# Attention, cosine network and top-1 experts: the gate in column groups, the sinks as one product, the masks first

## The chip, the cores and the metric

The kernel runs on one core of one Trainium2 chip. The metric is the device time of an execution in microseconds (us), as the median of several runs. Five engines work side by side, each on its own queue of instructions: PE multiplies matrices (PEld is its weight load), DVE, ACT and POOL work on vectors, and SP starts transfers.

## What is computed

```python
def _attn_ref(q, k, v, n_sink, window):          # 4 batches, 8 heads, 768 x 64
    scores = scale * np.matmul(q, k.transpose(0, 1, 3, 2))
    keep = is_sink | in_window                   # 4 sinks, a window of 128
    scores = np.where(keep, scores, -1000000000.0)
    a = softmax(scores)
    return np.matmul(a, v)

x = attn_out.transpose(0, 2, 1, 3).reshape(3072, 512)
h = x @ w_in                                     # 512 -> 2048
x = (h * np.cos(h)) @ w_out                      # 2048 -> 512
logits = x @ w_gate + modality_bias[modality_id] # 8 experts
e_idx = np.argmax(logits, axis=1)
out[mask] = gate_w[mask, None] * (np.maximum(x[mask] @ w1[e], 0.0) @ w2[e])   # expert by expert
```

## The kernel before

Attention goes by half-batches hb = 0 to 7 of 384 queries (an even hb is the first half of its batch) and in each by 4 pairs of heads. `attn_front` (L395) makes a pair's generators. The front loads queries and keys, transposes them on PE and has ACT copy them out of PSUM (L450, L468). `mid` (L474) multiplies them (tile ps), lets DVE add the masks and find the maxima (L502), and ACT take exponents (L518). `rest` (L521) scales and transposes the probabilities (pt, pT) and multiplies them with the values into po. Window and sinks are apart there: the sinks' probabilities, 16 columns a head, are copied to pc (by POOL for the first half-batches, then by DVE, L573, L575), transposed into pz (L578), copied by ACT into sp (L579), and multiplied with the sinks' values vs_n, one product for each head, into the two halves of po's partitions (L592). From hb = 2 on (`whole`) this runs beside the first network; from hb = 3 (`STACK`) the scores are three products of split operands in fp32r.

The first network, `ffn_tile_gen` (L648), goes by tiles of 384 tokens and 16 blocks of 128 hidden columns: 12 matmuls hp with 384 columns, a cosine on DVE and ACT (ch), and 9 matmuls y with 512 columns, in fp32r, each operand split in a high and a low part (g_h and g_l, the latter made on POOL, L699). `conv_gen` (L274) builds such parts of the weights out of 64-bit inputs on ACT and DVE during the first 200 us.

For each finished tile of y, `route_tile` (L734) chooses the experts. For each of its 3 blocks of 128 tokens PE transposes the block (yT, L743), DVE copies it out, and PE multiplies it with the gate's weights: 4 products of 128 rows with 8 moving columns (pl, L754). These are woven between matmuls of the first network (`mmf`, L625). DVE adds the bias and goes on to ranks and lists. Eight tiles give 24 blocks. After it come the experts, in pages of 256 tokens, under branches (`run`, L1291).

A scheduler sorts the instructions of each engine by priority and dependences; edges between instructions (`add_manual_dep`) restrain it. The start of the program, L842 to L954, was written thus: front of the first pair, transfers of sinks and window (L849), masks (L886 to L904) and the routing's constants (L906 to L940), the first weight conversion, the rest of the first pair.

Of the kernel before, what the change touches and what calls it, by code (L numbers as in the profile page):

```python
# [11 lines left out]
F32 = DT.float32  # L12
# [45 lines left out]
CONV_LEAD = 8  # L58


@with_exitstack
def kernel(
# [178 lines left out]
    sp2 = [apool.tile([P, HALF], F32, name=f"sp{i}") for i in range(2)]  # L241
# [14 lines left out]

    def conv_bits(cpool, raw):
# [3 lines left out]
        ACT.activation(out=h, in_=hi.bitcast(F32), func=AF.Copy, scale=REBASE)  # L261
# [133 lines left out]
    def attn_front(hb, pr):  # L395
# [10 lines left out]

        vs_n, sp = vs_n2[pr % 2], sp2[pr % 2]
# [59 lines left out]
        else:  # L467
            ACT.activation(out=kT[0][:, 0:nblk, 0:P], in_=pk3[:, 0:nblk, :], func=AF.Copy)  # L468
# [52 lines left out]
        def rest():  # L521
# [47 lines left out]
            pc = apool.tile([P, NQ, 2, NS], F32, name="pc")  # L569
            if extra:  # L570
# [3 lines left out]
            else:  # L574
                (POOL if hb < NPOOL else DVE).tensor_copy(pc[:, t0:], Pt[:, t0:, :, P:SEG])  # L575
            pz = psb("pz")
            for t in range(t0, NQ):
                PE.transpose(pz[0:2 * NS, t * P:(t + 1) * P], pc[:, t].rearrange("p j s -> p (j s)"), ident)  # L578
            ACT.activation(out=sp[0:2 * NS, t0 * P:], in_=pz[0:2 * NS, t0 * P:HALF], func=AF.Copy)  # L579
# [11 lines left out]
            for j in range(2):  # L591
                mm(po[hr[j], t0 * P:HALF], vs_n[:, j * D:(j + 1) * D], sp[:, t0 * P:HALF], True, False)  # L592
# [27 lines left out]
    woven = []  # L620

    edge = mybir.DependencyInfo(mybir.DependencyClass.NoSync, mybir.DependencyReason.DATA)
    last_mm = [None]

    def mmf(o, l, r, start, stop):  # L625
        i = PE.matmul(o, l, r, start=start, stop=stop)  # L626
        if last_mm[0] is not None:
            tc.add_manual_dep(i.ins, last_mm[0].ins.name, edge, reason="woven")
            last_mm[0] = None
        if woven:  # L630
            last_mm[0] = woven.pop(0)()
            tc.add_manual_dep(last_mm[0].ins, i.ins.name, edge, reason="woven")

    def weave():
        if woven:
            woven.pop(0)()


# [9 lines left out]
    def ffn_tile_gen(ypool_of):  # L648
# [4 lines left out]
        def second(c):  # L653
# [6 lines left out]
            for t in range(NQ):  # L660
                yp = yps[i][t]
                s = slice(t * P, (t + 1) * P)
                mmf(yp, gh[:, s], oh, f == f0, False)
                mmf(yp, gh[:, s], ol, False, False)
                mmf(yp, gl[:, s], oh, False, f == f1 - 1)
# [68 lines left out]
    def route_tile(i, yp):  # L734
# [3 lines left out]
        lg = yp.tile(s3, F32, name="lg")  # L738
        for t in range(NQ):
# [4 lines left out]
            yT = yp.tile([P, KD, P], F32, name="yT", bufs=1)  # L744
            DVE.tensor_copy(yT.rearrange("p c x -> p (c x)"), pt)
            yield 0
            for _ in range(4 if i < NTILE - 2 else 0):
                yield 0
            pl = []

            def gate(c):
                if c == 0:
                    pl.append(ps_a("pl"))
# [4 lines left out]
            while woven:  # L758
                weave()
            tt(DVE, lg[:, t, :], pl[0][:, 0:NE], bias_all[:, t0 + t, :], ALU.add)  # L760
            if t < NQ - 1:
                continue
            yield 0
# [78 lines left out]
    first = attn_front(0, 0)  # L842
    next(first)
    next(first)

# [3 lines left out]
    SP.dma_start(out=rt[:, 0:2], in_=n_sink.partition_broadcast(P).squeeze(1))  # L849
    SP.dma_start(out=rt[:, 2:4], in_=window.partition_broadcast(P).squeeze(1))  # L850
# [15 lines left out]
    bad = tmpc.tile([P, 2], F32, name="bad")  # L866
    ts(DVE, bad[:, 0:1], ns_c, float(NS), ALU.is_gt)
    ts(DVE, bad[:, 1:2], win_c, float(P), ALU.is_gt)
    tt(DVE, bad[:, 0:1], bad[:, 0:1], bad[:, 1:2], ALU.add)
    ts(DVE, bad[:, 1:2], win_c, 1.0, ALU.is_lt)  # L870
    tt(DVE, bad[:, 0:1], bad[:, 0:1], bad[:, 1:2], ALU.add)
    bad_i = const.tile([P, 1], I32, name="bad_i")
    DVE.tensor_copy(bad_i, bad[:, 0:1])


    iota_i = tmpc.tile([P, NV], I32, name="iota_i")
    POOL.iota(iota_i, pattern=[[1, NV]], base=0, channel_multiplier=0)
    iota_f = const.tile([P, NV], F32, name="iota_f")
    DVE.tensor_copy(iota_f, iota_i)
    prow_i = tmpc.tile([P, 1], I32, name="prow_i")  # L880
    POOL.iota(prow_i, pattern=[[0, 1]], base=0, channel_multiplier=1)
    cols2 = const.tile([P, 2], F32, name="cols2")
    prow, half_pi = cols2[:, 0:1], cols2[:, 1:2]
    DVE.tensor_copy(prow, prow_i)

    masks = const.tile([P, 3, W3], BF16, name="masks")  # L886
    rel = tmpc.tile([P, P], F32, name="rel")
    sk = tmpc.tile([P, P], F32, name="sk")
    mw = tmpc.tile([P, P], F32, name="mw")
    ts(DVE, rel, iota_f[:, 0:P], prow, ALU.subtract, -1.0, ALU.mult)  # L890
    ts(DVE, sk, iota_f[:, 0:P], ns_c, ALU.is_lt)
    POOL.memset(masks, 0.0)

# [10 lines left out]
    ts(DVE, masks, masks, -1.0, ALU.add, -NEG / SCALE, ALU.mult)  # L904

    sides = const.tile([P, 2, P], BF16, name="sides")  # L906
    ts(DVE, sides[:, 0], rel, 0.0, ALU.is_gt)
    ts(DVE, sides[:, 1], rel, 0.0, ALU.is_le)
    tri = const.tile([P, P], BF16, name="tri")
    ones = const.tile([P, P], BF16, name="ones")  # L910
    ts(DVE, tri, rel, 0.0, ALU.is_lt)
    DVE.memset(ones, 1.0)
    DVE.memset(half_pi, HALF_PI)

    wg = const.tile([P, KD, NE], F32, name="wg")
# [478 lines left out]
```

## Time and profile before

| | |
|---|---|
| three runs | 1146.69, 1145.22, 1146.74 us; median 1146.69 |
| the profiled execution | 1143.94 us, its span 1142.2 |
| PE busy | 1103.6 us, 97% of the span, 6624 matmuls |
| DVE, ACT, POOL busy | 678.3 us (59%), 602.5 (53%), 224.5 (20%) |
| mean granted clock of PE | 0.996 |

Busy time is the union of an engine's instructions. Those of PE overlap in the records, so what one costs is read from the start of one to the start of the next. Line numbers are those of the kernel before. Idle time of an engine costs something only where others wait for it.

### The profile page before, as it was taken

How to read it: one execution, taken by the hardware profiler on the slowest of the kernel's cores; microseconds unless marked ns; L12 is line 12 of the kernel's file. 1: busy time of each engine (PE TensorE's matmuls, PEld its weight loads, DVE VectorE, ACT ScalarE, POOL GpSimd, SP SyncE). 2: the span in 40 equal slices, each digit the busy share in tenths (PEclk: the TensorE clock that was granted, in tenths of full speed). 3: DMA queues.
4: the chain of work that ended last, by engine and by line, in shares of the span. 5: the costliest groups of instructions: out<-in, count | busy, mean ns of one | idle time of the engine just before them, and what ended most of it. 6: DMA issues, size and time to landing. Idle time of an engine off the chain costs nothing.

```text
span 1142.2 us, 20840 instructions
## 1 busy us (share of the span) xinstructions
PE 1103.6 (97%) x6624; PEld 928.0 (81%) x6624; DVE 678.3 (59%) x2126; ACT 602.5 (53%) x1239; POOL 224.5 (20%) x273
## 2 busy tenths in 40 slices
PE   5989999999999999999999999999999999999995
PEld 3667777888888878888888879999889998899984
DVE  6778888666876766776676774746742125522210
ACT  5878887656665566665657553434322225422221
POOL 1232224211111111111111111322121211221110
PEclk9999999999999999999999999999999999999998
DMA  6567665422332322323233223633151115111110
GB/s 150 151 197 196 195 195 158 109 73 68 95 74 76 105 72 64 108 70 75 63 104 79 62 75 102 230 93 89 60 203 40 57 58 184 41 58 39 40 43 23
DMA packets 136083, 113.40 MB, mean 99 GB/s; under 512 B 95727, under 2 KB 103919, under 8 KB 135920
## 3 DMA queue, kind: packets, MB, share of 16 engines
q1 hardware_dynamic: 131600, 97.87, 30.3%
q0 software_dynamic: 4320, 13.65, 3.7%
q8 instruction: 66, 1.08, 0.4%
q14 instruction: 97, 0.79, 0.2%
HBM read 151.06 MB, written 19.67 MB: 149 GB/s over the span
## 4 chain that ended last, share of the span: by engine, by line
PE 85%; DVE 5%; DMA 5%; ACT 2%; issue 1%; POOL 1%; SPq 0%; DVEq 0%; POOLq 0%; ACTq 0%
PE hp L136 23%; PE y L626 22%; PE m_h L136 10%; PE m_y L136 10%; PE ps L136 5%; PE po L136 5%; DMA out_dram<-m_ot,m_ids 3%; DMA cv_in<-in_moe_w_in_dram 1%; PE pl L754 1%; PE pq L444 1%; PE pt L546 1%; PE yT L743 1%; PE pk L454 1%; PE m_a L1093 1%; PE mh L136 1%
## 5 line engine op out<-in xcount | busy, mean ns | idle before, releaser
L148 POOL TENSOR_TENSOR g_l<-ch,g_h 128x384 fp32r<-128x384 f32 x128 | 132.4, 1035 | 558.2 <-ACT g_h L698 435.4
L136 PE MATMUL hp<-xT_h,wi_h 128*128 128x384 f32 x512 | 188.3, 368 | 2.7 <-DVE ch L148 2.7
L136 PE MATMUL hp<-xT_h,wi_l 128*128 128x384 f32 x512 | 174.5, 341 | 0.0
L136 PE MATMUL hp<-xT_l,wi_h 128*128 128x384 f32 x512 | 174.0, 340 | 0.0
L626 PE MATMUL y<-wo,g_h 128*128 128x512 f32 x384 | 158.6, 414 | 0.0
L626 PE MATMUL y<-wo_l,g_h 128*128 128x512 f32 x384 | 155.6, 405 | 0.0
L626 PE MATMUL y<-wo,g_l 128*128 128x512 f32 x384 | 154.1, 401 | 0.2 <-POOL g_l L148 0.2
L688 ACT ACTIVATE ch<-ch,cols 128x384 f32<-128x384 f32 x128 | 78.7, 616 | 116.6 <-DVE ch L145 116.0
L136 PE MATMUL m_y<-wi_h,hT 128*128 128x512 f32 x416 | 132.5, 393 | 0.7 <-ACT m_ot L1135 0.6
L145 DVE SCALAR_TENSOR_TENSOR hT<-m_h,hT 128x256 fp32r<-128x256 f32 x88 | 37.3, 424 | 151.0 <-ACTq L1287 102.4
L136 PEld LDWEIGHTS hp<-xT_h,wi_h 128*128 128x128 f32 x512 | 96.7, 189 | 18.1 <-issue 7.2
L142 DVE TENSOR_SCALAR ch<-hp 128x384 int32<-128x384 f32 x128 | 70.9, 554 | 59.1 <-PE hp L136 46.3
L698 ACT ACTIVATE g_h<-ch 128x384 fp32r<-128x384 f32 x128 | 66.4, 520 | 67.8 <-DVE ch L148 46.0
L136 PEld LDWEIGHTS hp<-xT_l,wi_h 128*128 128x128 f32 x512 | 97.0, 189 | 3.7 <-issue 0.2
L136 PEld LDWEIGHTS hp<-xT_h,wi_l 128*128 128x128 f32 x512 | 96.7, 189 | 1.2 <-issue 0.9
L148 DVE TENSOR_TENSOR ch<-ch,hp 128x384 f32<-128x384 f32 x128 | 70.4, 550 | 39.9 <-ACT ch L688 39.5
L136 PEld LDWEIGHTS m_y<-wi_h,hT 128*128 128x128 f32 x416 | 78.1, 188 | 17.0 <-issue 1.0
L518 ACT ACTIVATE Pb<-Pb,mx 128x272 f32<-128x272 f32 (+1 forms) x168 | 82.9, 494 | 10.9 <-DVE mx L502 10.0
L626 PEld LDWEIGHTS y<-wo,g_l 128*128 128x128 f32 x384 | 72.2, 188 | 14.8 <-POOL g_l L148 0.8
L626 PEld LDWEIGHTS y<-wo,g_h 128*128 128x128 f32 x384 | 72.4, 189 | 13.8 <-issue 3.3
L502 DVE CUSTOM_DVE_ANT_0 Pb<-ps,masks 128x272 f32<-128x272 f32 (+1 forms) x168 | 63.7, 411 | 31.7 <-PE ps L136 31.2
L136 PE MATMUL ps<-kT,qT 64*128 64x272 f32 (+1 forms) x504 | 72.6, 350 | 8.9 <-ACT kT L468 7.0
(276 smaller groups left out, 2236.0 us busy)
## 6 DMA issues: line engine op xcount, KB each, us to landing
rw<-in_moe_w_dram SPq DMA_DIRECT2D x112, 512.0 KB
wo_l<-wl_scr SPq DMA_DIRECT2D x122, 256.0 KB
cv_in<-in_moe_w_in_dram SPq DMA_DIRECT2D x16, 512.0 KB
cv_out<-in_moe_w_out_dram SPq DMA_DIRECT2D x16, 512.0 KB
y_scr<-yt SPq DMA_DIRECT2D x24, 256.5 KB
xT_h<-xg_h SPq DMA_DIRECT2D x32, 192.0 KB
xT_l<-xg_l SPq DMA_DIRECT2D x32, 192.0 KB
qn<-in_q_dram SPq DMA_DIRECT2D x56, 96.0 KB
```

Source lines behind the costliest of these rows:

```text
L136: PE.matmul(o, l, r, start=start, stop=stop)
L142: e.tensor_scalar(out=o, in0=i, scalar1=s1, scalar2=s2, op0=op0, op1=op1)
L145: e.scalar_tensor_tensor(out=o, in0=i0, scalar=s, in1=i1, op0=op0, op1=op1)
L148: e.tensor_tensor(out=o, in0=a, in1=b, op=op)
L444: PE.transpose(pq[:, t * P:(t + 1) * P], qn[:, t].rearrange("p j d -> p (j d)"), ident)
L454: PE.transpose(pk[:, t * P:(t + 1) * P], kn[:, t].rearrange("p j d -> p (j d)"), ident)
L502: DVE.tensor_tensor_reduce(out=Pb[t][j][:, c0:c1], in0=ps[j][:, 0:w], in1=masks[:, min(half * NQ + t, 2), c0:c1], scale=-SCALE, scalar=3.0 ...
L518: ACT.activation(out=Pb[t][j][:, c0:c1], in_=Pb[t][j][:, c0:c1], func=AF.Exp, scale=-1.0, bias=mx[:, i:i + 1], accum_out=sm[:, i:i + 1])
L546: PE.transpose(pt2[:, j * P:(j + 1) * P], Pb[t][j][:, SEG:W3], ident)
L626: i = PE.matmul(o, l, r, start=start, stop=stop)
L688: ACT.activation(out=ch, in_=ch, func=AF.Sin, scale=TWO_PI, bias=half_pi)
L698: ACT.activation(out=gh, in_=ch, func=AF.Copy)
```

## The change

It has three parts, and a small fourth.

The gate: a tile's three transposed blocks go into one tile yT of 4 x 384 columns. The weights are widened to 32 columns with zeros and become the stationary side: four fp32 products with 384 moving columns, each into 32 partitions of one PSUM tile (pg). ACT copies that out, and three products with 8 columns against a matrix of ones (gsum) add up the four parts and turn them. Weaving goes.

The sinks, for hb from 2 on: DVE splits pc into high, high and low parts (96 rows after the transpose), POOL makes high, low and high parts of the values, and one fp32r product of all 128 columns gives what two fp32 products gave.

The start: masks ahead of all other work on DVE, in a fixed order; the sinks' and window's words loaded by ACT; the first pair finished behind the masks; the first conversion on ACT behind the first keys; all other constants behind half-batch 0.

The fourth: the hint of an expert page's branch goes to ACT and DVE too.

```diff
+            if whole:
+                pc = apool.tile([P, NQ, 3, 2, NS], F32R, name="pc3")
+                pv = Pt[:, t0:, :, P:SEG]
+                DVE.tensor_copy(pc[:, t0:, 0:2], pv.unsqueeze(2).to_broadcast([P, NQ - t0, 2, 2, NS]))
+                tt(DVE, pc[:, t0:, 2], pv, pc[:, t0:, 0].bitcast(F32), ALU.subtract)
+                vsr = vsr2[pr % 2]
+                i0, i1, i2 = [slice(i * 2 * NS, (i + 1) * 2 * NS) for i in range(3)]
+                POOL.tensor_copy(vsr[i0], vs_n[i0])
+                POOL.tensor_copy(vsr[i2], vs_n[i0])
+                tt(POOL, vsr[i1], vs_n[i0], vsr[i0].bitcast(F32), ALU.subtract)
...
-            ACT.activation(out=sp[0:2 * NS, t0 * P:], in_=pz[0:2 * NS, t0 * P:HALF], func=AF.Copy)
+            ACT.activation(out=sp[0:nr, t0 * P:], in_=pz[0:nr, t0 * P:HALF], func=AF.Copy)
...
-            for j in range(2):
+            if whole:
+                mm(po[:, t0 * P:HALF], vsr2[pr % 2], sp[:, t0 * P:HALF], True, False)
+            for j in range(0 if whole else 2):
                 mm(po[hr[j], t0 * P:HALF], vs_n[:, j * D:(j + 1) * D], sp[:, t0 * P:HALF], True, False)
...
-                mmf(yp, gh[:, s], oh, f == f0, False)
+                mm(yp, gh[:, s], oh, f == f0, False)
...
-            DVE.tensor_copy(yT.rearrange("p c x -> p (c x)"), pt)
+            DVE.tensor_copy(yT[:, :, t * P:(t + 1) * P], pt.rearrange("p (c x) -> p c x", x=P))
             yield 0
...
-                return PE.matmul(pl[0][:, 0:NE], yT[:, c, :], wg[:, c, :], start=c == 0, stop=c == KD - 1)
-
-            woven.extend([lambda c=c: gate(c) for c in range(KD)])
...
+        pg_ = ps_a("pg")
+        for c in range(KD):
+            mm(pg_[c * GW:(c + 1) * GW, 0:HALF], wg[:, c, :], yT[:, c, :], True, True)
+        gs = yT[:, 0, :]
+        ACT.activation(out=gs, in_=pg_[:, 0:HALF], func=AF.Copy)
+        yield 0
+        pl = ps_a("pl")
+        for t in range(NQ):
+            mm(pl[:, t * NE:(t + 1) * NE], gs[:, t * P:(t + 1) * P], gsum, True, True)
+        tt(DVE, lg, pl[:, 0:NQ * NE].rearrange("p (t e) -> p t e", e=NE), bias_all[:, t0:t0 + NQ, :], ALU.add)
...
-    SP.dma_start(out=rt[:, 0:2], in_=n_sink.partition_broadcast(P).squeeze(1))
-    SP.dma_start(out=rt[:, 2:4], in_=window.partition_broadcast(P).squeeze(1))
+    ACT.dma_start(out=rt[:, 0:2], in_=n_sink.partition_broadcast(P).squeeze(1))
+    ACT.dma_start(out=rt[:, 2:4], in_=window.partition_broadcast(P).squeeze(1))
...
+    made = DVE.tensor_scalar(out=masks, in0=masks, scalar1=-1.0, scalar2=-NEG / SCALE, op0=ALU.add, op1=ALU.mult)
+    mine = [i_ for i_ in nc.cur_bb.bb.instructions[at_:] if i_.engine == made.ins.engine]
+    for a_, b_ in zip(mine, mine[1:]):
+        tc.add_manual_dep(b_, a_.name, nosync, reason="masks in this order")
+
+    with tc.issue_after(made.ins):
+        first = attn_front(0, 0)
...
+        next(conv)
+        fronts[0, 0][0]()
...
+    with tc.issue_after([i_ for i_ in nc.cur_bb.bb.instructions if i_.engine == made.ins.engine][-1]):
+        sides = const.tile([P, 2, P], BF16, name="sides")
...
-                tc.mark_branch_hint_location(f"full{T + 1}", hint=flags[T + 1, "full"], engines=(ET.PE,))
+                tc.mark_branch_hint_location(f"full{T + 1}", hint=flags[T + 1, "full"], engines=(ET.PE, ET.Activation, ET.DVE))
```

Three places show how instructions move. The first is DVE's queue at the program's start, before: `rel`, `sk` and `mw` are masks in the making, `m`, `btmp`, `sides` and `tri` constants of the routing and of later half-batches, `ks` the first pair's sink keys.

```order
L140 TENSOR_SCALAR sk<-iota_f,lim 128x128
L142 TENSOR_SCALAR rel<-iota_f,cols_198 128x128
L148 TENSOR_TENSOR btmp<-m_233,mb 128x192
L140 TENSOR_SCALAR mw<-rel,lim 128x128
L903 CAST masks<-sk 128x16
L140 TENSOR_SCALAR sides<-rel 128x128
L145 SCALAR_TENSOR_TENSOR mw<-rel,mw 128x128
L458 COPY ks<-pk 128x16
L896 CAST masks<-mw 128x128
L897 CAST masks<-mw 128x128
L148 TENSOR_TENSOR masks<-mw,sk 128x128
```

After the change, in the same place, down to the first reduction of scores:

```order
L900 CAST masks<-mw 128x128
L149 TENSOR_TENSOR masks<-mw,sk 128x128
L902 CAST masks<-sk 128x16
L903 TENSOR_SCALAR masks<-masks 128x816
L472 COPY ks<-pk 128x16
L141 TENSOR_SCALAR bad<-lim 128x1 x2
L149 TENSOR_TENSOR bad<-bad 128x1
L141 TENSOR_SCALAR bad<-lim 128x1
L149 TENSOR_TENSOR bad<-bad 128x1
L486 COPY kT<-pk 128x2x16
L924 CAST bad_i<-bad 128x1
L518 ISA Pb,mx<-ps,masks 128x128
```

The masks stand without constants between them, and the first pair's keys and the test of the inputs (`bad`) behind them.

The second is DVE's queue at the end of half-batch 0, before, where `xs` is the last pair's scaling and `pb_x` a reduction of half-batch 1's scores:

```order
L502 ISA Pb,mx<-ps,masks 128x272
L502 ISA mx 128x1
L148 TENSOR_TENSOR xs<-po,xs 128x384
L145 SCALAR_TENSOR_TENSOR cv_a<-cv_h,cv_a 128x512
L140 TENSOR_SCALAR sm<-sm 128x6
L470 COPY kT<-ks 128x3x16
L563 RECIPROCAL sm<-sm 128x6
L145 SCALAR_TENSOR_TENSOR cv_a<-cv_out,cv_a 128x512
L502 ISA pb_x_98,mx<-ps,masks 128x272
L502 ISA mx 128x1
```

After:

```order
L149 TENSOR_TENSOR xs<-po,xs 128x384
L141 TENSOR_SCALAR sides<-rel 128x128 x2
L141 TENSOR_SCALAR tri<-rel 128x128
L951 MEMSET ones 128x128
L956 CAST m_1097<-mid 128x24
L143 TENSOR_SCALAR tok_1103<-iota_f 128x24
L967 MEMSET wg 128x4x24
L143 TENSOR_SCALAR m_1097<-m_1097 128x24
L149 TENSOR_TENSOR btmp<-m_1097,mb 128x192
L149 TENSOR_TENSOR bias_all<-m_1097,mb 128x192
L141 TENSOR_SCALAR tok_1103<-tok_1103,cols_161 128x24
L149 TENSOR_TENSOR bias_all<-bias_all,btmp 128x192
```

The constants have come in between, as one block.

The third is PE's queue behind the last tile of the first network, before, where `mh` are matmuls of the first expert's page:

```order
L136 MATMUL mh<-m_xT_l,wi_h_79 128x256
L754 MATMUL pl<-wg,yT 128x8 x4
L136 MATMUL mh<-m_xT_h,wi_l_89 128x256
L136 MATMUL mh<-m_xT_h,wi_h_80 128x256
L136 MATMUL mh<-m_xT_l,wi_h_80 128x256
L743 MATMUL yT<-ident,yt 128x128 x4
L136 MATMUL mh<-m_xT_h,wi_l_90 128x256
L136 MATMUL mh<-m_xT_h,wi_h_81 128x256
L754 MATMUL pl<-wg,yT 128x8 x4
L136 MATMUL mh<-m_xT_l,wi_h_81 128x256
L136 MATMUL mh<-m_xT_h,wi_l_91 128x256
```

After:

```order
L137 MATMUL mh<-m_xT_l,wi_h_81 128x256
L137 MATMUL mh<-m_xT_h,wi_l_91 128x256
L137 MATMUL pg<-yT,wg 32x384 x4
L137 MATMUL mh<-m_xT_h,wi_h_78 128x256
L137 MATMUL mh<-m_xT_l,wi_h_78 128x256
L137 MATMUL mh<-m_xT_h,wi_l_88 128x256
L137 MATMUL mh<-m_xT_h,wi_h_79 128x256
L137 MATMUL mh<-m_xT_l,wi_h_79 128x256
L137 MATMUL pl<-gsum,yT 128x8 x3
L137 MATMUL mh<-m_xT_h,wi_l_89 128x256
```

Three groups of four small products (the rows show two of them) have become four wide ones and three small ones, with five matmuls between.

## Rows read from the trace of the kernel before

**Rows 1.** Two stretches: busy us (instructions) of PE, PEld, DVE, ACT, POOL; clock, DMA share, GB/s
```profile
200.00:700.00 500.00, 498.58 (x3024) 413.23 (x3024) 346.22 (x1154) 307.28 (x604) 86.45 (x85) 1.00 0.31 83
830.00:1142.00 312.00, 295.61 (x1847) 265.19 (x1846) 93.43 (x260) 89.30 (x193) 54.01 (x51) 0.99 0.22 72
```

**Rows 2.** Timeline of the start: start us, us, engine, line, operation, tiles, idle before
```profile
3.36 0.43 SPq L850 DMA_DIRECT2D rt<-in_window_dram  x1
...
5.21 0.88 PE L454 MATMUL pk<-ident,kn 128*128 128x128 f32 x3
5.34 2.80 SPq L249 DMA_DIRECT2D cv_in<-in_moe_w_in_dram  x2
7.01 0.17 DVE L852 CAST rf<-rt 128x4 f32<-128x4 int32 x1 [5.47 <-DMA rt<-in_window_dram]
...
11.58 0.66 ACT L261 ACTIVATE cv_h<-cv_in 128x512 f32<-128x512 f32 x1 [9.54 <-DMA cv_in<-in_moe_w_in_dram]
...
12.52 0.48 ACT L468 ACTIVATE kT<-pk 128x384 f32<-128x384 f32 x1
...
13.05 1.08 PE L136 MATMUL ps<-kT,qT 64*128 64x128 f32 x4 [6.96 <-ACT kT L468]
13.14 0.36 DVE L142 TENSOR_SCALAR masks<-masks 128x816 bf16<-128x816 bf16 x1
...
14.92 0.28 DVE L502 CUSTOM_DVE_ANT_0 Pb<-ps,masks 128x128 f32<-128x128 f32 x1
```

**Rows 3.** Timeline of PE round one gate block of the last tile
```profile
817.49 0.28 PE L136 MATMUL mh<-m_xT_h,wi_h 128*128 128x256 f32 x1
817.61 0.96 PE L754 MATMUL pl<-wg,yT 128*128 128x8 f32 x8
818.43 0.36 PE L136 MATMUL mh<-m_xT_l,wi_h 128*128 128x256 f32 x1
818.63 0.28 PE L136 MATMUL mh<-m_xT_h,wi_l 128*128 128x256 f32 x1
```

**Rows 4.** Timeline of PE round the sinks of an odd half-batch's pair
```profile
225.23 0.39 PE L626 MATMUL y<-wo_l,g_h 128*128 128x512 f32 x1
225.46 0.40 PE L626 MATMUL y<-wo,g_l 128*128 128x512 f32 x1
225.79 0.87 PE L136 MATMUL po<-sp,vs_n 128*64 128x384 f32 x4
226.49 1.47 PE L136 MATMUL po<-pT,vn 128*64 128x128 f32 x16
227.88 0.45 PE L136 MATMUL hp<-xT_h,wi_h 128*128 128x384 f32 x1
228.17 0.34 PE L136 MATMUL hp<-xT_l,wi_h 128*128 128x384 f32 x1
228.34 0.33 PE L136 MATMUL hp<-xT_h,wi_l 128*128 128x384 f32 x1
```

**Rows 5.** Timeline of PE at the sinks of an even half-batch's pair
```profile
131.09 0.44 PE L136 MATMUL po<-sp,vs_n 128*64 128x128 f32 x4
131.36 1.03 PE L136 MATMUL po<-pT,vn 128*64 128x256 f32 x6
```

**Rows 6.** Timeline of PE at the first cosines
```profile
66.20 0.44 PE L136 MATMUL hp<-xT_h,wi_h 128*128 128x384 f32 x1 [2.73 <-DVE ch L148]
...
67.03 0.52 PE L136 MATMUL hp<-xT_l,wi_h 128*128 128x384 f32 x1
67.35 0.52 PE L136 MATMUL hp<-xT_h,wi_l 128*128 128x384 f32 x1
```

**Rows 7.** The tiles pc and g_l: instructions, ns min/median/max, first and last start
```profile
L575 DVE COPY pc<-Pb x20: 181/194/226, 221.1 to 681.6; 128x96 f32<-128x96 f32 x12, 128x32 f32<-128x32 f32 x8
...
L575 POOL COPY pc<-Pb x8: 208/212/349, 21.5 to 194.8; 128x32 f32<-128x32 f32 x6, 128x96 f32<-128x96 f32 x2
...
L148 POOL TENSOR_TENSOR g_l<-ch,g_h x128: 995/1012/1549, 67.1 to 809.2; 128x384 fp32r<-128x384 f32 x128
```

More of the change, by code (lines that the diff above doesn't have):

```diff
@@ L240 @@
     vs_n2 = [apool.tile([P, 2 * D], F32, name=f"vs_n{i}") for i in range(2)]
-    sp2 = [apool.tile([P, HALF], F32, name=f"sp{i}") for i in range(2)]
+    sp2 = [apool.tile([P, HALF], F32, name=f"sp{i}", tag=f"sp{i}") for i in range(2)]
+    vsr2 = []
     for i in range(2):
@@ L260, in conv_bits @@
         h = cpool.tile([P, 512], F32, name="cv_h", bufs=2)
-        ACT.activation(out=h, in_=hi.bitcast(F32), func=AF.Copy, scale=REBASE)
+        i_ = ACT.activation(out=h, in_=hi.bitcast(F32), func=AF.Copy, scale=REBASE)
+        if front_act:
+            tc.add_manual_dep(i_.ins, front_act[-1].ins.name, nosync, reason="behind the first keys")
+            front_act.clear()
         h = h.bitcast(I32)
@@ L405, in folded @@
             return whole and (half == 1 or t > 1)
+        if whole and not vsr2:
+            for i in range(2):
+                vsr2.append(apool.tile([P, 2 * D], F32R, name=f"vs_r{i}"))
+                sp2[i] = apool.tile([P, HALF], F32R, name=f"sp_r{i}", tag=f"sp{i}")
+                POOL.memset(vsr2[i].bitcast(F32), 0.0)
+                POOL.memset(sp2[i].bitcast(F32), 0.0)
         vs_n, sp = vs_n2[pr % 2], sp2[pr % 2]
@@ L467, in attn_front @@
         else:
-            ACT.activation(out=kT[0][:, 0:nblk, 0:P], in_=pk3[:, 0:nblk, :], func=AF.Copy)
+            i_ = ACT.activation(out=kT[0][:, 0:nblk, 0:P], in_=pk3[:, 0:nblk, :], func=AF.Copy)
+            if hb == 0 and pr == 0:
+                front_act.append(i_)
             src = pk3[:, 0:1, 0:NS] if half == 0 else ks[:, pr, 0:1, :]
@@ L848 @@
     rt = tmpc.tile([P, 4], I32, name="rt")
-    SP.dma_start(out=rt[:, 0:2], in_=n_sink.partition_broadcast(P).squeeze(1))
-    SP.dma_start(out=rt[:, 2:4], in_=window.partition_broadcast(P).squeeze(1))
+    ACT.dma_start(out=rt[:, 0:2], in_=n_sink.partition_broadcast(P).squeeze(1))
+    ACT.dma_start(out=rt[:, 2:4], in_=window.partition_broadcast(P).squeeze(1))
+    iota_i = tmpc.tile([P, NV], I32, name="iota_i")
+    POOL.iota(iota_i, pattern=[[1, NV]], base=0, channel_multiplier=0)
+    prow_i = tmpc.tile([P, 1], I32, name="prow_i")
+    POOL.iota(prow_i, pattern=[[0, 1]], base=0, channel_multiplier=1)
+    masks = const.tile([P, 3, W3], BF16, name="masks")
+    POOL.memset(masks, 0.0)
+    at_ = len(nc.cur_bb.bb.instructions)
+    iota_f = const.tile([P, NV], F32, name="iota_f")
+    DVE.tensor_copy(iota_f, iota_i)
+    cols2 = const.tile([P, 2], F32, name="cols2")
+    prow, half_pi = cols2[:, 0:1], cols2[:, 1:2]
+    DVE.tensor_copy(prow, prow_i)
+    rel = tmpc.tile([P, P], F32, name="rel")
+    sk = tmpc.tile([P, P], F32, name="sk")
+    mw = tmpc.tile([P, P], F32, name="mw")
+    ts(DVE, rel, iota_f[:, 0:P], prow, ALU.subtract, -1.0, ALU.mult)
     rf = tmpc.tile([P, 4], F32, name="rf")
@@ new lines @@
+    mine = [i_ for i_ in nc.cur_bb.bb.instructions[at_:] if i_.engine == made.ins.engine]
[3 more added lines that the diff above has]
+        first = attn_front(0, 0)
+        for _ in first:
+            pass
+        mids.add((0, 0))
+        for _ in fronts[0, 0][1]():
+            pass
+        next(conv)
+        fronts[0, 0][0]()
+        bad = tmpc.tile([P, 2], F32, name="bad")
+        ts(DVE, bad[:, 0:1], ns_c, float(NS), ALU.is_gt)
+        ts(DVE, bad[:, 1:2], win_c, float(P), ALU.is_gt)
+        tt(DVE, bad[:, 0:1], bad[:, 0:1], bad[:, 1:2], ALU.add)
+        ts(DVE, bad[:, 1:2], win_c, 1.0, ALU.is_lt)
+        tt(DVE, bad[:, 0:1], bad[:, 0:1], bad[:, 1:2], ALU.add)
+        bad_i = const.tile([P, 1], I32, name="bad_i")
+        DVE.tensor_copy(bad_i, bad[:, 0:1])
```

152 lines of the change are left out of this document (53 added, 99 removed).

## The prediction

> **What bounds the kernel now.** I read the table by stretches first. Between 200 and 700 us PE is busy for 498.6 of 500 us, DVE for 346, ACT for 307, POOL for 86 [rows 1]. Attention and the first network share PE there, and the other engines have a third of their time free: what leaves PE shortens this stretch, what is added to the others is covered. In the last 312 us, the experts, PE is busy for 295.6 [rows 1]; none of the changed matmuls are there. Then the timeline of the first 16 us: PE ends its transposes of the first keys at 6.1, and does nothing until 13.05, when ACT has copied them out [rows 2]. ACT could have copied at 6.1; it stood at the first weight conversion, whose data landed at 11.58 [rows 2]. Even without that, the first scores wait for the masks, which DVE ends at 13.5 among other constants; the first reduction reads them at 14.92 [rows 2].
>
> PE is charged here by start to start, since its durations overlap: a y matmul of 512 columns takes 0.23 us, an hp matmul of 384 columns 0.17 [rows 4].
>
> **Gate.** Before, 24 blocks of 4 products with 8 moving columns. Each is in fp32 and runs as two instructions. Four of them in a row stand between the mh that starts at 817.49 and the one at 818.43; the eight take 0.82 us, and the mh behind takes 0.20 where its kind takes 0.12 [rows 3]. So (0.82 + 0.08) / 4 = 0.225 us each, 96 x 0.225 = 21.6 us. The transposes and copies ahead of them stay in number.
>
> After, each of 8 tiles has four fp32 products of 384 columns, one in each quarter of the array's columns, an ACT copy, and three 8-column products. For the four there is no row; the nearest is the sink product of before, two fp32 products of 384 columns in two halves of the array. Their four instructions start at 225.79 and the next product at 226.49, so 0.70; the y ahead takes 0.33 instead of 0.23, and the first hp behind the fp32 block 0.29 instead of 0.17 [rows 4]. One fp32 product alone must stream its columns four times, 4 x 0.17 = 0.68, so the two heads ran at once. If four quarters run as two halves do, a tile costs 0.70 + 0.10 + 0.12 + 3 x 0.225 = 1.6 us, 12.8 in all: **8.8 us less**. Bounds: none at once, 4 x 0.68 = 2.7 plus the rest 0.9, is 3.6 a tile, 28.8, and 7.2 us more than before; below 12.8 I see nothing. I take the lower, since the row of the two halves is the nearest in form.
>
> The trace shows 0.70 for two halves and nothing of four [rows 4]. [...]
>
> The ACT copies (8 of 384 columns, 0.48 us each as the keys' copy [rows 2]) and the six more table loads that ACT's order holds lie beside PE in a stretch where ACT is busy 61% [rows 1]. DVE saves 16 small additions. Without that cover each tile would wait for its ACT copy, some 0.7 us.
>
> **Sinks.** In 24 pairs (half-batches 2 to 7) two fp32 products become one in fp32r, with 96 of 128 rows in use. In the 12 pairs of odd half-batches they have 384 columns: 0.70 + 0.10 for the switch [rows 4]. The new product has hp's shape and type, 0.17, and the switch moves behind it, 0.10: 0.53 less, 6.3 us. In the 12 of even ones they have 128 columns: 0.27 from 131.09 to 131.36 [rows 5]. For 128 columns in fp32r there is no row; between a third of hp (0.06) and all of it (0.17) I take 0.11: 0.16 less, 1.9 us (1.2 to 2.5). Together **8.2 us less**.
>
> Added: one small DVE subtraction beside the copy, which was 0.19 and grows a little [rows 7]; 24 x 0.25 = 6 us on DVE, covered (69% busy [rows 1]), but in the chain from the softmax to the transposes of pz. POOL gets three small operations a pair, 0.6 us at the 0.21 of its small copies [rows 7], 15 us over a stretch where it is busy 17% [rows 1]; queued behind them is g_l, 1.0 us each [rows 7], which y needs. I cost both at nothing; if the cover is missing, PE stands at pz or po for what is late.
>
> **The start.** The two words with sinks and window are issued by ACT first, at about 1.2 us instead of 3.36 behind four loads [rows 2]. DVE got them at 7.01 [rows 2], so at about 4.9 now. Behind that stand 19 mask operations in place of the 36 that DVE issued between 7.01 and 13.14 [rows 2], 0.17 each: masks at 4.9 + 19 x 0.2 = 8.7, allowing for their larger size. Eight small ones follow, so the first reduction is at 10.2 or 10.4 in place of 14.92: 4.5 us earlier. The keys are out of PSUM at 6.7, since the conversion now stands behind. On SP the two conversion loads move up from 5.34 to 2.8; the next pair's queries follow eight shorter loads and reach PE in time, or up to 1 us late.
>
> But 18 DVE constants that stood in idle time now stand, in one block, behind the last xs of half-batch 0. At 0.17 that is 3.1 us at about 55 us, shortly before PE waits 2.73 us for DVE's end of the cosine chain, until 66.20 [rows 6]. Cost: 0 if the idle times take it, 3.1 if none do; I take 1.5. [...] The start is worth 4.5 - 1.5 = **3 us less** (0 to 4.5).
>
> **Hints.** ACT and DVE now get a hint of each expert page's branch, as PE has. PE's idle time in the whole last stretch is 16.4 us [rows 1], most of it the last page's way out. I put 0, with 1 us to either side.
>
> **Sum.** 8.8 + 8.2 + 3.0 = 20.0 us. The profiled execution took 1143.94 (span 1142.2 and 1.7 around it) and would take 1123.9. It is 2.75 under the median of the three runs, 1146.69, so the median becomes 1126.7; I say **1127 us**, -1.7%.
>
> **Rivals.**
> 1. *The quarters do not run at once.* Each product is two instructions, and the program has both of a quarter ahead of the next quarter's. If PE kept to that order, the second would hold up the next quarter: 2.7 instead of 0.70 a tile, 8 x 2.0 = 16 us, giving 1143, which is just faster than 0.2%. In pairs it would be 1.4, so 5.6 us and 1132.5. For it: no four have been seen. Against: the two heads of rows 4 stand in the program in just that way, and take 0.70, not 1.37. [...] In pairs 9%, one by one 4%.
> 2. *Another engine sets the pace.* Attention's exponents, the cosine and the splits follow an order that was laid for a longer PE time. If half of the 17 us stays as new short waits, the median is 1135. For it: ACT has six more table loads, and the chain to pz is longer. Against: 150 to 190 us of DVE and ACT are free between 200 and 700 [rows 1]. 13%.
> 3. *Slower: the sinks' chain stops PE.* PE takes its instructions in order. If DVE's second operation, or POOL's copies caught behind g_l (1.0 us) [rows 7], come late, pz or po stands, and hp and y with it. It decides against the change from 20 us / 24 = 0.83 us a pair; one g_l ahead of the copies, 1.0, gives 24 less 20, so 1151; two give 1175. Against: POOL is 17% busy and its copies need only the sinks' values, loaded long before. 6%.
> 4. *The start's gain is taken back whole* (the constants at 55 us, or the second pair's loads): 1130, 12%.
> [...]
>
> **How the numbers follow.** The forecast with rival 5 has 56%, its own range 1120 to 1131; rivals 1 to 4 have 13, 13, 6 and 12. The range must hold 8 in 10: from 1118 (all unknown costs at their best) to 1138, which takes in the pairs of rival 1, rival 2 and rival 4. A measurement of this kernel tells 0.2%, 2.3 us, from no change. Slower by that needs rival 3, or a mixture of 1 and 2: 7%. Within it falls part of rival 1 at its worst and of 2: 5%. Faster: 88%.
>
> **What would show it.** The four quarter products start within a few hundredths of each other, and the next starts some 0.7 behind: the gate is right. In the sink block one product stands 0.17 ahead of the first po of values. The first reduction of scores starts at about 10.3 instead of 14.92. The wait before the first cosine at 66 us says what the block of constants cost. PE's busy time should fall by 17 us, and its idle time by 3. The forecast is wrong if PE's idle time grows between 130 and 830 us, above all ahead of pz and po, or if the quarter products take over 1.4 us.

## The result, and the profile after

The change made the kernel **slower**: 1152.83 us median (1149.7 to 1154.25) against 1146.01 (1144.48 to 1148.19), ratio 1.0051, 95% interval 1.0038 to 1.0064. The prediction was 1127; it gave a slower kernel 7%. The profiled execution has a span of 1147.9 us. PE's busy time, forecast to fall by 17 us from 1103.6, rose by 2:

```profile
PE 1105.7 (96%) x6472; PEld 921.2 (80%) x6472; DVE 683.4 (60%) x2142; ACT 614.3 (54%) x1253; POOL 253.3 (22%) x345
```

The stretches of the kernel after. The columns are those of [rows 1]: busy us (instructions) of PE, PEld, DVE, ACT, POOL, then the granted clock.

```profile
60.00:130.00 70.00, 66.86 (x379) 50.29 (x378) 58.20 (x153) 59.00 (x127) 26.74 (x46) 0.93 0.62 182
130.00:200.00 70.00, 66.42 (x323) 49.41 (x321) 56.29 (x151) 51.31 (x105) 24.22 (x37) 0.95 0.61 182
200.00:700.00 500.00, 496.41 (x2941) 407.07 (x2940) 355.06 (x1188) 322.17 (x629) 108.48 (x148) 1.00 0.31 83
830.00:1148.00 318.00, 301.86 (x1887) 272.00 (x1885) 98.08 (x284) 90.48 (x196) 54.51 (x52) 0.98 0.21 71
```

The first two stretches of the kernel before:

```profile
60.00:130.00 70.00, 65.43 (x393) 50.10 (x392) 56.82 (x141) 61.07 (x131) 21.46 (x41) 0.98 0.72 206
130.00:200.00 70.00, 68.82 (x374) 52.11 (x373) 59.92 (x157) 55.55 (x114) 21.43 (x32) 1.00 0.59 176
```

From 60 to 200 us PE starts 702 matmuls where it started 767, and its granted clock is 0.93 and 0.95 in place of 0.98 and 1.00. Set side by side by the same hp matmul, the kernel after is 1.6 us behind at the first one (39.3 before), 13.0 behind at the 289th (220.3 before), and 7.1 behind near 803. So 13 us are lost in the first 220, and behind that only 6 of the 17 are won that gate and sinks were to bring.

The start, in answer to [rows 2]:

```profile
9.34 0.49 ACT L482 ACTIVATE kT<-pk 128x384 f32<-128x384 f32 x1 [2.04 <-DVE ks L472]
...
10.71 0.29 DVE L518 CUSTOM_DVE_ANT_0 Pb<-ps,masks 128x128 f32<-128x128 f32 x1 [0.53 <-PE ps L137]
...
16.02 0.87 PE L458 MATMUL pq<-ident,ld_x 128*128 128x128 f32 x3 [1.83 <-DMA ld_x<-in_q_dram]
...
22.77 0.69 DVE L146 SCALAR_TENSOR_TENSOR cv_a<-cv_h,cv_a 128x512 int32<-128x512 int32 x1 [3.64 <-DVEq L161]
...
22.84 0.66 PE L572 MATMUL pt<-ident,Pb 128*128 128x128 f32 x2 [3.92 <-DVEq L161]
```

The first reduction is at 10.71, 4.2 us earlier, near the 4.5 forecast. Then PE waits 1.83 us for the second pair's queries, and 3.92 at L161, the branch to the general path (DVEq is DVE's sequencer). Before, PE waited 0.30 at that place:

```profile
20.93 0.66 PE L556 MATMUL pt<-ident,Pb 128*128 128x128 f32 x2 [0.30 <-DVE ks L458]
```

The first product of values (into po, with the sinks' values) is at 30.71, 2.5 later than before.

Gate and sinks, in answer to [rows 3] and [rows 4]:

```profile
256.83 0.40 PE L137 MATMUL y<-wo,g_l 128*128 128x512 f32 x1
257.16 0.85 PE L137 MATMUL pg<-yT,wg 128*32 128x384 f32 x8
257.94 0.44 PE L562 MATMUL pt<-ident,Pb 128*128 128x128 f32 x2
...
239.15 0.34 PE L137 MATMUL po<-sp_r,vs_r 128*128 128x384 f32 x1
239.41 1.52 PE L137 MATMUL po<-pT,vn 128*64 128x128 f32 x16
```

The eight instructions of the four quarters take 0.78 us. The sinks' product stands 0.26 ahead of the first values where two took 0.70.

### The profile page after: what moved, and what is told of

It reads as the page before. It is cut to its first block, busy times and chain, and to the rows that moved or that the text cites. A ratio compares the mean times of both kernels' runs of the same rounds, so it can differ in the third digit from the quotient of the medians.

```text
span 1147.9 us, 20666 instructions
## 1 busy us (share of the span) xinstructions
PE 1105.7 (96%) x6472; PEld 921.2 (80%) x6472; DVE 683.4 (60%) x2142; ACT 614.3 (54%) x1253; POOL 253.3 (22%) x345
## 3 DMA queue, kind: packets, MB, share of 16 engines
q8 instruction: 64, 1.05, 0.4%
## 5 line engine op out<-in xcount | busy, mean ns | idle before, releaser
L137 PE MATMUL y<-wo_l,g_h 128*128 128x512 f32 x384 | 152.6, 397 | 0.8 <-DMA wo_l<-wl_scr 0.8
L137 PE MATMUL ps<-kT,qT 64*128 64x272 f32 (+1 forms) x504 | 80.8, 355 | 6.5 <-ACT kT L482 3.0
```

## The experiments

The first theory (A) was that the moved start loses the time, the rivals that gate and sinks give back theirs (B, C). Medians in us; the kernel before ran beside each group. The ratios on record are not the quotients of the medians and differ from them by up to 2 us; where it matters, both are given.

| kernel | median | ratio to before, 95% |
|---|---|---|
| gate alone | 1146.08 | 0.9982, 0.9964 to 1.0001 |
| sinks alone | 1150.00 | 1.0013, 0.9996 to 1.0030 |
| start alone | 1154.51 | 1.0062, 1.0041 to 1.0083 |
| gate and sinks | 1142.28 | 0.9952, 0.9933 to 0.9971 |
| sinks, parts on POOL | 1143.76 | 0.9975, 0.9960 to 0.9989 |
| change, SP's later loads behind the branch | 1157.02 | 1.0084, 1.0060 to 1.0108 |
| the same, constants' loads too | 1151.93 | 1.0049, 1.0030 to 1.0068 |
| change, constants ahead of the branch | 1144.55 | 0.9979, 0.9961 to 0.9998 |
| gate and sinks, parts on POOL | 1140.97 | 0.9942, 0.9924 to 0.9960 |
| change, constants and parts | 1142.34 | 0.9966, 0.9944 to 0.9989 |
| gate and sinks, parts on POOL, light start | 1150.82 | 1.0031, 1.0009 to 1.0053 |
| gate and sinks, parts on POOL, routing spread | 1134.39 | 0.9897, 0.9875 to 0.9918 |
| gate and sinks, parts on POOL, yT copied by ACT | 1145.26 | 0.9993, 0.9979 to 1.0008 |
| start alone, constants ahead of the branch | 1154.63 | 1.0066, 1.0043 to 1.0088 |
| gate alone, routing spread | 1138.13 | 0.9928, 0.9907 to 0.9949 |
| change, constants, parts and spread | 1140.20 | 0.9946, 0.9929 to 0.9962 |

**One part at a time.** The hunks of the diff, each part alone; gate and sinks together on the old start.

> The kernel before with the gate's edit alone: quarters, one ACT copy, the sum of four; the sums' matrix is made among the old constants. Theory A (the moved start loses the time, the gate does what was forecast): 8.8 us under the kernel before, ratio 0.992. Theory B (gate and sinks give back part of their gain in new waits and split groups, since attention's order was laid for a longer PE): 3 to 5 us under it, 0.996 to 0.997. Theory C (the sinks' edit is what loses): as A.

> The kernel before with the sinks' edit alone: three stacked parts, one product. Theory A (the moved start loses the time): 8.2 us under the kernel before, 0.993. Theory B (short new waits): 3 to 5 us under it. Theory C (the sinks' longer chain or POOL's three operations stop PE): no gain or slower, 1.000 to 1.006, with idle time ahead of pz or po from 130 us on.

> The kernel before with the moved start alone; gate and sinks are the old ones, ACT and DVE get no new hints. Theory A: the branch behind the first pair stops all engines for some 3.9 us, the order of the next 200 us is worse for it, and the run is 10 to 18 us slower, 1.009 to 1.016. Theories B and C: the stop of 3.9 us takes back the 4.2 us that the first scores come earlier, and the total is within 3 us of the kernel before.

> Gate and sinks together on the old start, no new hints. Theory A: 17 us under the kernel before, 0.985, near 1129. Theory B: 6 to 10 us under it, 0.991 to 0.995. Theory C: no faster than 1.000.

By the ratios the parts give -2.1, +1.5 and +7.1 us, in sum +6.5; the whole change +5.8. None gives its term, and the intervals of the gate and of the sinks reach no change. That the sums agree does not show that the parts add: gate and sinks together give -5.5, where their own two make -0.6. The start comes nearest to theory A (7 us, under its 10 to 18). The gate falls short of theory B, the sinks lie where theory C had them (1.000 to 1.006), and gate and sinks together just miss theory B's lower end.

**The sinks: DVE waits for POOL.** In half-batch 2 POOL normalises the attention weights, and in the kernel before it also made the copy pc; the change gave pc to DVE in every half-batch from 2 on. The sinks alone, PE's wait and DVE's row:

```profile
133.17 0.44 PE L136 MATMUL hp<-xT_h,wi_h 128*128 128x384 f32 x1 [1.35 <-DVE ch L148]
```
```profile
132.23 0.20 DVE L579 CAST pc<-Pb 128x64 fp32r<-128x64 f32 x1 [2.28 <-POOL Pb L142]
132.46 0.19 DVE L148 TENSOR_TENSOR pc<-Pb,pc 128x32 fp32r<-128x32 f32 x1
132.57 0.55 DVE L148 TENSOR_TENSOR ch<-ch,hp 128x384 f32<-128x384 f32 x1
```

DVE stands 2.28 us until POOL is done, and the cosine's step for which PE waits is queued behind. From 126 to 232 us DVE has three such waits, 6.5 us in all, and the kernel after has the same (us in all, times, longest):

```profile
DVE pc L588 <- POOL Pb L143: 6.5, 3, 2.2
PE hp L137 <- DVE ch L149: 2.1, 1, 2.1
```

The edit, on the sinks alone, with arguments left out:

```diff
-DVE.tensor_copy(pc[:, t0:, 0:2], ...)
-tt(DVE, pc[:, t0:, 2], pv, ...)
+e_ = POOL if hb < NPOOL else DVE
+e_.tensor_copy(pc[:, t0:, 0:2], ...)
+tt(e_, pc[:, t0:, 2], pv, ...)
```

> The sinks' edit alone, but in half-batch 2, where POOL normalises the weights, POOL also makes the three parts, as it made the copy in the kernel before. Theory A (with the parts on DVE, DVE stands 6.5 us in three pairs of half-batch 2 for POOL's normalising, and PE then stands 1.4 us for DVE's cosine chain): DVE has no wait for POOL there, PE's 1.4 us are gone, the first matmul at 200 us comes 3 to 6 us earlier than with the sinks' edit alone, and the time is 1144 to 1147. Rival (these 10 us are the clock's and chance): the waits go, the time stays within 2 us of the sinks' edit alone, 1148 to 1152.

Measured: 1143.76, 6.2 us under the sinks alone by the medians, 4.4 by the ratios; PE's wait and DVE's waits for POOL are gone, and the matmul at 197.8 before is 3.9 late in place of 10.9. In the same stretch DVE's row is now:

```profile
127.81 0.55 DVE L148 TENSOR_TENSOR ch<-ch,hp 128x384 f32<-128x384 f32 x1 [0.52 <-ACT ch L713]
```

Theory A holds. Part of the 7.0 us between 10.9 and 3.9 is half speed of TensorE: the sinks alone lose 5.1 us to it from 40 to 320 us, this kernel 1.7 (the sum of one minus the granted clock over windows of 1 us, as below).

**The branch.** All engines pass the branch; which one makes PE wait? The first idea was SP, whose queue has five loads more ahead of it. With `held` the SP instructions behind the branch in the program and `meet` the branch's end (the second run holds back `held[0:3]` too):

```diff
+for i_ in held[11:]:
+    tc.add_manual_dep(i_, meet.name, nosync, ...)
```

> The changed kernel, with SP's loads for the third pair and all that follow held behind the branch at which all engines meet. Theory A (the engines wait there for SP, whose queue has five loads more ahead of the branch): PE's wait of 3.9 us near 22.8 falls to under 1.2, the first product of values comes at 27 to 28.5 instead of 30.7, and the time falls by some 3 us, to 1150. Rival (the branch itself costs 3.9 us, whenever SP comes): the wait stays at 3 to 4 us and so does the time.

> As the run before it, and the gate's weights, bias and modality words also go behind the branch on SP. Theory A (those three loads hold the second pair's queries up on SP): the wait of 1.8 us near 16.0 goes as well, the first product of values comes at 25 to 27, and the time is 4 to 6 us under the changed kernel, 1147 to 1149. Rival (the transfers of the conversion's loads hold the queries up): that wait stays over 1 us.

Measured: 1157.02 and 1151.93. SP passes at 17.06 in place of 21.57, and PE still waits:

```profile
23.36 0.66 PE L572 MATMUL pt<-ident,Pb 128*128 128x128 f32 x2 [4.54 <-DVEq L161]
...
23.30 0.69 DVE L146 SCALAR_TENSOR_TENSOR cv_a<-cv_h,cv_a 128x512 int32<-128x512 int32 x1 [4.26 <-DVEq L161]
```

Theory A falls: not SP. The second run's queries did not come in time either: PE's order had them ahead of the first scores, at 13.72, and the first reduction slid back to 14.93. What differs is DVE: its next instruction starts 3.06 us behind its own branch in the kernel after, 3.69 here, 0.60 before; 57 rows of DVE stand ahead of the branch now, 71 before. So the constants were put back ahead of it, in the changed kernel and in the start alone (the moved lines in words):

```diff
+wg, mb, mid loads and the constants, behind the masks
 bad_r = nc.values_load(...)
 general_attention()
-wg, mb, mid loads
 for n_, _ in enumerate(attn_half(0)):
     conv_to(int(CONV_A * n_))
-the constants
```

> The changed kernel, with the routing's constants (and the loads they need) put back ahead of the branch, behind the masks; 15 more of DVE's instructions stand ahead of the branch. Theory A (DVE goes on 3.1 us behind its branch in the changed kernel, 0.6 in the kernel before, because what it jumps to is fetched only then: an 8 KB instruction transfer starts at 20.7, behind the branch, where before it started at 18.4, ahead of it): DVE goes on 0.6 behind its branch, PE's wait of 3.9 us falls under 1, the first product of values comes at 26.5 to 28.5 instead of 30.7, and the time falls by 3 to 6 us, to 1147 to 1150. Rival (the engines wait for each other there): PE's wait stays over 2.5 us.

> The moved start alone, old gate and sinks, with the constants put back ahead of the branch. Theory A (the unprepared branch of DVE and what follows from it are the start's loss): 1145 to 1149 against 1146.8 before and 1154.5 for the moved start alone. Rival (the earlier first scores run into the second pair's loads and lose there, whatever the branch does): 1151 to 1155.

DVE goes on 0.71 us behind its branch. PE's waits, in the changed kernel and in the start alone:

```profile
21.46 0.66 PE L572 MATMUL pt<-ident,Pb 128*128 128x128 f32 x2 [1.75 <-DVEq L161]
```
```profile
19.27 0.66 PE L564 MATMUL pt<-ident,Pb 128*128 128x128 f32 x2 [0.40 <-ACT Pb L526]
```

That DVE's wait hangs on the instructions ahead of the branch is shown: in the five profiles with 57 rows ahead it is 2.87 to 3.69 us, in the fifteen with 66 to 75 it is 0.59 to 0.71. That what DVE jumps to is fetched late is the reading that fits. The packets that carry instructions agree. In each of the fifteen, one of 8 KB starts between 12.9 and 17.1 us, ahead of DVE's branch; four of the five have none there, and the fifth has one 1.1 us behind SP's branch. In all twenty another starts 1.0 to 1.8 us behind DVE's branch. In the fifteen DVE has gone on by then; in the five it goes on 1.9 to 2.1 us later (20.73 and 22.67 in the kernel after). No row names the engine that a packet serves, so this stays a reading.

The time is another matter. The changed kernel fell by 8 us, but its first product of values came at 32.4, between the 30.7 and 34.0 of two profiles of the kernel after, and the start alone stayed where it was. At the first hp matmul the profiles with the moved start are 4.5 to 6.6 us behind the kernel before, with the wait or without it (one profile of the kernel after is only 1.6 behind), and those with the old start, the light start below aside, from 0.1 ahead to 2.9 behind. The branch does not settle the start's loss.

**Half speed.** Two kernels ran again, unchanged.

> The kernel before, a second profile. Theory A (where TensorE falls to half speed is a matter of chance from one execution to the next): the stretch of half speed near 66 to 71 us is missing or elsewhere, and the first hp matmul and the one at 200 us shift by 1 to 4 us. Rival (it belongs to the kernel): the stretch is there again within half a microsecond, 1.7 us lost in all.

> The changed kernel, a second profile. Theory A (its stretches at half speed belong to the kernel, as they did in the second profile of the kernel before): the same four stretches near 63, 121, 135 and 187 us within a microsecond, 8 to 9 us lost. Rival (chance): 2 to 5 us lost, in other places.

Half speed is a granted clock of 0.50; under it the kernel before starts its hp matmuls 0.32 us apart in place of 0.17. The kernel before lost 1.7 us both times, at 67 to 70. The kernel after lost 8.6 and 6.8: near 64 (69 the second time), 122 and 187 both times, near 135 once; that is neither theory as it stood. With the constants ahead of the branch the profile lost nothing, and that is as much as its 8 us; the start alone lost 3.4, with the constants 5.1.

The mean granted clock of every run says the same. It is 0.987 to 0.990 in the six runs of the kernel after, and 0.991 to 0.997 in the 93 of the kernel before in the groups above. One minus the clock, times the span, is on average 13.8 us a run against 6.3, and 7.2 with the constants ahead of the branch. So half speed takes some 7 us more in the kernel after, as much as its whole slowdown, though some of it passes while PE stands idle; and most of the 8 us that the constants gave back is half speed.

What makes the clock fall is not shown. Ahead of most falls PE stood idle for 0.6 to 2.8 us, and waits of the same size pass without one: the 2.8 us at 66.9 in the gate alone, 1.5 at 125.9 with the constants. The kernel after also fell at 971.6, with no wait over 0.2 us in the 7 us ahead. At the very start the column for the clock says 1.00, and yet the transposes are at half speed. Before, and after (second profile):

```profile
25.33 0.27 PE L556 MATMUL pt<-ident,Pb 128*128 128x128 f32 x1
25.44 0.27 PE L555 MATMUL pt<-ident,Pb 128*128 128x128 f32 x1
```
```profile
32.58 0.42 PE L572 MATMUL pt<-ident,pb_x 128*128 128x128 f32 x1
32.79 0.42 PE L571 MATMUL pt<-ident,pb_x 128*128 128x128 f32 x1
```

They start 0.11 apart at full speed, 0.21 at half. The last ones at half speed start at 21.8 in both profiles before, at 25.5 and 33.0 after, at 32.7 with the start alone and 30.1 with its constants ahead of the branch. But the old start has such late cases too, 29.7 with the sinks alone and 30.0 with gate and sinks, and the changed kernel with constants and parts has 22.2, in spite of waits of 1.80 us at 16.0 and 1.75 at 20.6. So the late full speed is not the moved start's alone, and that its waits keep the clock down is not shown.

**Both mended, and a light start.**

> Gate and sinks on the old start, with the three parts made by POOL in half-batch 2. Theory A (the wait of DVE for POOL cost the sinks' edit 6 us and costs it as much beside the gate): 4 to 6 us under gate and sinks together, so 1136 to 1139, ratio 0.990 to 0.993. Rival (gate and sinks together had already hidden it): within 1.5 us of gate and sinks together, 1141 to 1143.

> The changed kernel with both: the constants ahead of the branch, and the parts on POOL in half-batch 2. Theory A (the two losses are the main ones and add up): 1152.8 less 4 less 6, so 1141 to 1145, faster than the kernel before. Rival (the moved start loses elsewhere too, by the order of the first 200 us): 1146 to 1150.

The light start moves only the two words to ACT and the first conversion behind the first keys:

> Gate and sinks with the parts on POOL, on the old start, of which only two things change: ACT issues the two words, and the first conversion stands behind the first keys' copy. Theory A (an earlier first score is worth its time as long as the branch and the loads stay where they were): first reduction 2 to 3 us earlier than 14.9, and 1 to 3 us under the kernel without it. Rival (the first 60 us are bound by the loads and DVE, so an earlier score is given back): within 1 us of it.

Gate and sinks with the parts on POOL: 1140.97, 1.3 under gate and sinks, so the rival holds (the two medians come from different groups). The changed kernel with both: 1142.34, inside theory A. The light start lost 10 us, which neither theory had: first scores at 11.3, the first reduction at 14.1 and so only 0.8 earlier, then waits of 1.6 and 1.4 us for the second pair and at the branch, full speed lost from 37 to 51 (in the profile, of a run of 1153.84 us; the ten go from 1146.66 to 1156.96).

**The gate: half the steps.** The gate alone won 2 of 8.8. The trace has the block where it was lost, DVE and PE of the gate alone:

```profile
260.75 0.38 DVE L143 TENSOR_SCALAR rB<-iota_f,rpg,tok 128x192 fp32r<-128x192 f32 x1
261.04 1.05 DVE L141 TENSOR_SCALAR rA<-iota_f,rrank 128x128 fp32r<-128x128 f32 x1
262.01 0.37 DVE L143 TENSOR_SCALAR rB<-iota_f,rpg,tok 128x192 fp32r<-128x192 f32 x1
262.31 0.28 DVE L141 TENSOR_SCALAR rA<-iota_f,rrank 128x128 fp32r<-128x128 f32 x1
262.50 0.37 DVE L143 TENSOR_SCALAR rB<-iota_f,rpg,tok 128x192 fp32r<-128x192 f32 x1
262.79 0.43 DVE L503 CUSTOM_DVE_ANT_0 Pb<-ps,masks 128x272 f32<-128x272 f32 x1
```
```profile
262.43 0.64 PE L137 MATMUL ps<-kT,qT 64*128 64x272 f32 x3
263.29 0.64 PE L137 MATMUL ps<-kT,qT 64*128 64x272 f32 x3 [0.21 <-DVE mx L503]
```

The routing's one-hot products (rA, rB) stand on DVE ahead of the score reduction, and PE's scores, six instructions that take 0.57 us in one stretch when the routing is spread as below (259.64 to 260.21), are split in two and take 1.42 (262.43 to 263.85). A step is a `yield`, at which the generator of the routing lets other work in. Before, a tile's routing had 19 steps up to its logits, 6 for each of its three transposes; the change left 9, so that this chain falls on attention's scores. Spread anew, to 18:

```diff
 DVE.tensor_copy(yT[:, :, t * P:(t + 1) * P], ...)
 yield 0
+for _ in range(3 if i < NTILE - 2 else 0):
+    yield 0
```

> Gate and sinks on the old start with the parts on POOL (1141.0), and the routing of a tile spread over as many steps as before: three empty steps behind each of the three copies of transposed rows. Theory A (the routing's copies and its chain on DVE now come in half the steps and hold up the score reductions that PE waits for): the three scores that wait for DVE near 262, 454 and 645 us go, and the time is 2 to 4 us shorter, 1137 to 1139. Rival (attention's own order on DVE was laid for a longer PE and is late by itself): within 1.5 us of 1141.0.

> Gate and sinks on the old start with the parts on POOL (1141.0), and ACT instead of DVE copies the transposed rows, 24 copies of 0.69 us. Theory A (DVE is late where PE waits, so 16 us less on DVE pay): 1 to 3 us shorter. Rival (ACT is as close to its limit, and the exponents come later): same within 1 us, or slower by up to 3.

> The kernel before with the gate's edit alone, and the routing of a tile spread over as many steps as before. Theory A (the fewer steps of the routing took back what the gate gave): 1146.7 less 7 to 9, so 1137.5 to 1140, with PE's waits for DVE near 263, 455 and 645 us gone. Rival (spreading pays only together with the sinks' edit): 1142 to 1146.

Measured: 1134.39, 6.6 under the same kernel without it (5.2 by the ratios), more than theory A had; the gate alone so is 8.3 us under the kernel before by the ratio, so the steps pay without the sinks too. Giving the copies to ACT made it 4 us slower: its rival holds, and by more than it had. PE's scores and transposes from 230 to 830 us (busy, mean ns, idle before and for what), the gate alone and then spread:

```profile
L137 PE MATMUL ps<-kT,qT 64*128 64x272 f32 (+1 forms) x342 | 39.2, 315 | 0.6 <-DVE mx L503 0.6
L547 PE MATMUL pt<-ident,Pb 128*128 128x128 f32 x82 | 16.4, 279 | 1.0 <-DVE qT L149 0.8 <-DVE kT L149 0.2
L579 PE MATMUL pz<-ident,pc 128*32 128x128 f32 x41 | 7.6, 272 | 0.8 <-DVE pc L576 0.8
```
```profile
L137 PE MATMUL ps<-kT,qT 64*128 64x272 f32 (+1 forms) x342 | 36.0, 316 | 0.0
L547 PE MATMUL pt<-ident,Pb 128*128 128x128 f32 x82 | 16.0, 276 | 0.0
L579 PE MATMUL pz<-ident,pc 128*32 128x128 f32 x41 | 7.7, 273 | 0.0
```

**What the start is worth.** All three mends on the changed kernel:

> The changed kernel with the constants ahead of the branch, the parts on POOL in half-batch 2, and the routing spread over as many steps as before. Theory A (the moved start by itself is worth nothing or loses, since PE then stands for the second pair's loads and stays at half speed longer): 1135 to 1141, slower than the same on the old start, 1134.4. Rival (the start's gain appears once the rest is mended): 1130 to 1134.

Measured: 1140.20, where the old start has 1134.39. Theory A holds by the medians. The two profiles do not show its reason: the moved start is 3.5 us behind at the first hp matmul and 0.1 at the 289th, and both reach the experts at 806 us (806.3 and 806.4). The 3.8 us between the two profiles lie in the experts (329.9 us against 326.0), where of the change only the hints act.

## Why the prediction was wrong

**Gate.** The term was right. A tile takes 0.10 (y ahead) + 0.78 + 0.05 to 0.11 (behind) + 0.59 for the three small products + 0.09 (the y behind them) = 1.6 to 1.7, as summed, and with the steps restored 8.3 us are won against 8.8. What failed is the step that said "the transposes and copies ahead of them stay in number" and stopped there: their number stayed, their spacing halved. From the 289th hp matmul to the last, PE spends 32.0 us on scores before and 35.7 with the gate alone, charged from start to start; with the steps restored it is 32.0. This is rival 2, which had 13%; its 8 us are near the 5 to 8 that the steps gave back, but it did not say where. The order of DVE was in the diff, in the empty steps.

**Sinks.** The step that failed is "I cost both at nothing". The row of pc on POOL [rows 7] runs to 194.8, so half-batch 2's copies stood there, behind POOL's normalising, and were moved to an engine that must wait for it. Rival 3 named DVE's second operation and POOL's copies; it was the first operation, and its input. Undone, it gives back 6.2 us by the medians, 4.4 by the ratios, when the sinks stand alone; beside the gate, 1.3.

The size was too high as well, for even so the sinks alone win only 3 us. An odd pair's block went from 0.79 to between 0.27 and 0.37 (0.27 forecast), an even one's from 0.37 to 0.15, and the first product of values behind it now takes 0.05 more. With the parts on POOL, 20 pairs win 4.9 us between the 289th hp matmul and the last, where the forecast's terms make 12 x 0.53 + 8 x 0.16 = 7.6. At the 289th that kernel is 3.0 us behind the kernel before, 1.4 of them already at the first.

**Start.** The step "4.5 - 1.5" failed in its first number. The first reduction came 4.2 us earlier, and the step counted that lead as time won; at the first product of values it had become 2.5 us of delay. What PE does next was not priced: the queries of the second pair at 16.0, and the branch at 22.8. The forecast weighed the queries ("up to 1 us late", 1.83 measured) and not the branch, although it moved 18 of DVE's instructions past it. The second number cost no visible wait near 55 us: the wait of 2.73 [rows 6] is gone and one of 1.15 ahead of a score stands there. Rival 4 had the mechanism of a gain taken back, and stopped at zero. Rival 5, which the 56% takes in, is a start that gains more than the forecast's 3 us; no run shows one: the start alone loses 7 us. The wait at the branch does not account for them, and the rest of the cause stays open.

**Half speed.** The sum has no term for it, though the hp matmuls at 67.03 and 67.35 [rows 6], behind the wait at 66 us, start 0.32 apart, and those of [rows 4] 0.17. In the kernel after 13.8 us a run are lost to it in place of 6.3. Why that changed is not shown.

**Hints.** From the first mh matmul to the end it is 327.7 to 331.0 us in seven profiles with the new hints, 326.0 to 330.6 in thirteen without: nothing beyond the spread, as forecast.

**Sum.** 26 us lie between forecast and result: about 7 at the gate, 10 at the sinks and 10 at the start, by the ratios of the parts alone, which do not strictly add. Cut the other way, some 7 of the 26 are half speed, which lies in several of the parts. Gate and sinks were judged from the stretch from 200 to 700 us, where the average leaves a third of DVE free; the losses lie in single places, some of them ahead of 230 us. Of the signs named at the end, idle time of PE did grow between 130 and 830 us, from 2.9 to 8.0 us, most of it ahead of pt, hp and pz. But that is the smaller part: the larger is that PE's busy time did not fall by 17 us.

Open: how the moved start loses time, alone and once all is mended, and what makes TensorE fall to half speed after some waits and not after others.

## What to carry to other kernels

When work leaves the busiest engine, count also the steps, slots or yields that it occupied: here they set where other engines' work falls, and putting them back was worth 5 to 8 us (with it, gate and sinks with the parts on POOL reach 1134.39, 1.0% under the kernel before, the best of all these). When an operation changes engine, look up in each stage who makes its input, and what is queued behind it. When work moves past a branch, count each engine's instructions ahead of it, and read the other waits between the moved step and the next thing PE can do. Before a lost microsecond is put down to an order, compare the granted clock of all runs.

## Of the hardware, not expected

Four fp32 products of 384 columns in the four quarters of the columns ran side by side: eight instructions in 0.78 us, against 0.70 for two halves [rows 4]. They start in two groups of four, 7 ns apart within a group and 0.33 us from one to the next. The halves of the kernel before start the same way, 7 ns apart (225.789 and 225.796), the second pair 0.37 later; so each of the two fp32 products has its half for 0.70, four times the 0.17 of an hp matmul with as many columns.

DVE's way on from a branch that is not taken into the general path took 0.6 to 0.7 us in fifteen profiles and 2.9 to 3.7 in five, which have fewer of DVE's instructions ahead of it (57 rows against 66 to 75). The page of the kernel after has instruction packets on two queues (packets, MB, share of 16 engines):

```profile
q8 instruction: 64, 1.05, 0.4%
q14 instruction: 100, 0.82, 0.2%
```

1.05 MB in 64 packets are 16 KB each, 0.82 in 100 are 8 KB each. No row says which engines they serve.
